# Turning normalised row tiles by transposing DMAs instead of array transposes and VectorE copies, with new planner tables

## The chip, the cores and the metric

The kernel runs on one core of one Trainium2 chip. Five engines work side by side, each through its own instructions in order: PE (TensorE, matmuls, with its weight loads shown as PEld), DVE (VectorE), ACT (ScalarE), POOL (GpSimd) and SP (SyncE, which here issues every DMA). The metric is the device time of one execution in microseconds, the median of several runs.

## The reference

Two layers of the same kind follow each other, with the same weights. Each adds softmax attention with 16 heads of width 28 to x, and then a feed-forward block with a squared relu; both read a layer norm of x without weights. x has 2048 rows of 448, the hidden width is 1792.

```python
x = x + _A_ref(_layernorm(x), A_wqkv, A_wo)
x = x + _B_ref(_layernorm(x), B_w1, B_b1, B_w2, B_b2)
x = x + _A_ref(_layernorm(x), A_wqkv, A_wo)
x = x + _B_ref(_layernorm(x), B_w1, B_b1, B_w2, B_b2)
# _A_ref: q, k, v = x @ wqkv; softmax(q @ k.T * 28**-0.5) @ v, per head; then @ wo
# _B_ref: relu(x @ w1 + b1)**2 @ w2 + b2
```

## The kernel before, in words

The 2048 rows are 16 row tiles of 128, mostly worked in blocks of two (256 rows). The attention is a long row of units: one unit is a score tile of 128 keys x r by 256 queries, 128x512 numbers in one PSUM bank, for one head. There are 2048 units in all. A score group (`s_stream`, matmuls at L1087) fills up to three banks of one of two PSUM buffers called sc, and one exp on ACT (`e_stream`, L1119) turns two or three banks of it into probabilities in `pts`. The matmuls at L1316 (`p_stream`) multiply them with V into oT.

Not all units go to ACT. Some are taken by DVE (`a_unit`, L1191: read the bank into v_w or K_sb), and the exponential is then worked out on POOL (L1216) and DVE (square at L1222, closing at L1255 in one instruction, or at L1243 after a further POOL instruction at L1231). I call this the side path. A unit of it takes 0.68 us of DVE for the first step alone, and the bank is not free for the next scores before that step is done.

Beside the units run the streams of the layers: for a finished block, the softmax's divisors go by small DMAs from SBUF (dn, L1420) to DRAM (scr, L1431) and back spread over rows (rec, L1439), the result is multiplied (L1444), projected and added to x (L1454), normalised, multiplied with w1 (relu L1512, square L1521) and w2, added, normalised again, and turned into the next layer's Q, K and V. All these matmuls but the transposes stand at L815 (`mm_tile`).

Each layer norm ends in the part that is changed. DVE writes the normalised row tile into one of four buffers xn (L779, two tiles make a pair, and two pairs take turns). PE transposes it, four 128x128 squares a tile, into a PSUM bank tp (L715), and DVE copies the bank into xnT (L727), where the features lie on the partitions and which is what L815 multiplies. xnT has three buffers; in the first layer's opening some blocks stand in K_sb of the other layer instead. PSUM is shared by two single banks (R_m), for which these transposes, the projections, the hidden layers and the oT sums stand in line. Where PE would have too little to do, `heat` (L1747) has it multiply ident with xn to no purpose.

The order on every engine is fixed when the program is built, by a planner (`Planner.run`): it keeps a clock for each engine, takes the operation that can start soonest, with priorities and with due times for scores and exps, and writes it into that engine's instructions. Tables of 128 numbers, one for each stretch of the run (OWN3, PACE, MIXT), decide how many units go to the side path, where in PSUM they lie, and which of the two closings they take. On the chip every engine then follows its own list, and a wait holds up all that stands behind it on that engine.

Of the kernel before, what the change touches and what calls it, by code (L numbers as in the profile page):

```python
# [14 lines left out]
P = 128  # L15
# [97 lines left out]
MIXT = (-9.0, 1.2, 1.2, -9.0, 1.2, 99.0, -9.0, 1.2, -9.0, 1.8, -9.0, -9.0, -9.0, 1.2, -9.0, 1.2, 1.8, -9.0, 1.8, 1.8, 1.2, 1.8, 1.8, -9.0, 1.2, 1.8, 1.2, -9.0, 1.2, -9.0, 1.2, 1.2, -9.0, -9.0, -9.0, 1.8, 1.8, -9.0, 1.8, -9.0, -9.0, -9.0, 1.2, 1.8, 1.2, 1.8, 1.8, -9.0, -9.0, 1.2, -9.0, 1.2, -9.0, 1.2, 1.2, -9.0, -9.0, -9.0, -9.0, -9.0, 1.2, 1.8, -9.0, -9.0, -9.0, 1.8, 1.2, 1.8, 1.2, -9.0, 1.2, 1.8, -9.0, 1.2, 1.2, 1.2, 1.2, 1.2, 1.8, -9.0, 99.0, 1.8, 99.0, 1.8, 99.0, 99.0, -9.0, 1.2, 1.2, 1.8, 1.8, 1.2, 1.2, 1.2, 1.8, 1.2, -9.0, 1.2, -9.0, -9.0, 1.8, 1.2, 1.2, 1.8, 1.8, 99.0, -9.0, 1.8, 99.0, -9.0, -9.0, -9.0, -9.0, 1.8, -9.0, 1.8, -9.0, 1.8, 1.8, 1.8, 1.2, -9.0, -9.0, 1.8, -9.0, -9.0, -9.0, -9.0)
# [20 lines left out]
EV = 2.9  # L134
# [244 lines left out]
def kernel(  # L379
# [12 lines left out]
    nc = tc.nc  # L392
    _, S, D = A_x.shape
# [27 lines left out]
    pl = Planner()  # L421
# [246 lines left out]
    def layernorm(t0, nt, deps_of, early=False, mv=None, place=None, x_in=None, parts=False):  # L668
# [34 lines left out]
        xnT = box["x"]  # L703
        ends = []
        todo = []

        def turn(p0, own, xs):
            box = {}

            def tr(e, xs=xs):  # L710
                tp = bank(t, "tp").bitcast(DT.bfloat16).rearrange("p (c q) -> p c q", c=NDC)
                box["t"] = tp
                for k, (xn, _) in enumerate(xs):
                    for dc in range(NDC):
                        nc.tensor.transpose(out=tp[:, dc, k * P:(k + 1) * P],  # L715
                                            in_=xn[:, dc * P:(dc + 1) * P], identity=ident[:, :])
            t = Op("PE", 0.07 * NDC * len(xs), tr, deps=[x[1] for x in xs],
                   acq=pools_now(early) if early else spare(1))
            yield t

            def ev(e, p0=p0, w=len(xs) * P):
                tp = box["t"]
                dst = xnT[:, :, p0 * P:p0 * P + w]
                if e == "ACT":
                    nc.scalar.copy(out=dst, in_=tp[:, :, 0:w])
                else:
                    return nc.vector.tensor_copy(out=dst, in_=tp[:, :, 0:w])  # L727
            o = Op("DVE", 0.15 + 0.265 * len(xs), ev, deps=[t], rel=t, sets=[("xT", t0 + p0)] if early else ())
            ends.append(o)
            pl.spawn(EV, iter([o, Op("DVE", 0.0, None, deps=[t], rel=own)]))  # L730

        if parts:
            own = Op("DVE", 0.0, None, acq=R_xn)
            yield own
            xn = xns[2 * (own.turn % 2)]
# [10 lines left out]
            for h, nm in enumerate(nms):  # L746
# [5 lines left out]
                t = Op("PE", 0.14, tr, deps=[nm], acq=spare(1) if h == 0 else None)  # L752
# [7 lines left out]
                o = Op("DVE", 0.28, ev, deps=[t], rel=box["o"])  # L760
# [5 lines left out]
        for p0 in range(0, nt, wide):  # L766
            js = range(p0, min(p0 + wide, nt))
            own = Op("DVE", 0.0, None, acq=R_xn)
            yield own
            xs = []  # L770
            for j in js:
                xn = xns[2 * (own.turn % 2) + j % 2]
# [16 lines left out]
            while todo:  # L789
                p0, own, xs = todo.pop(0)  # L790
# [158 lines left out]
    units = []  # L949
# [10 lines left out]
    at = [0]  # L960
# [60 lines left out]
    def s_stream():  # L1021
        while at[0] < len(units):
# [5 lines left out]
            def fn(e, gi=gi, us=us, js=js):  # L1028
# [174 lines left out]
    def a_rest(gi, c, box, unit):  # L1203
# [253 lines left out]
    def chain(l, qb):  # L1457
# [341 lines left out]
```

## Time and profile before

| | us |
|---|---|
| median of 3 runs | 809.45 (809.03 to 810.5) |
| span of the profiled execution | 808.2 |
| PE busy | 765.5 (95%) |
| DVE busy | 774.6 (96%) |
| ACT busy | 790.5 (98%) |
| POOL busy | 469.7 (58%) |

The profiled execution has a span of 808.2 us from its first instruction to its last; no time of its own beyond the span is given, and the runs are 0.8 to 2.3 us longer. In a row of the timeline the columns are start, duration, engine, line, operation and tiles; in brackets the engine's idle time before it and what ended that. In a group's row stand the count, the busy time and the mean duration of one in ns, and the idle time before. A row of waits has engine and line, the thing waited for, the total, the number of times and the longest, in us. A row of windows has, after the length, the busy time with the number of instructions for PE, PEld, DVE, ACT and POOL, then the clock, the DMA share and GB/s.

### The profile page before, as it was taken

What the parts mean: (1) busy time and instruction counts of PE and PEld (TensorE: products, weight loads), DVE (VectorE), ACT (ScalarE), POOL (GpSimd) and SP (SyncE); (2) the same over time, 40 slices, a digit from 0 to 9 for tenths busy, and PEclk for the clock granted to TensorE, in tenths of its full rate; (3) what the DMA queues carried; (4) which work ended last, traced back from release to release, by engine and by line L of the source; (5) the groups of instructions that cost most, each with busy time, mean ns of one, the idle gap of its engine ahead of it and who ended that gap; (6) DMA issues with size and microseconds to landing.
All of it is one profiled execution on the core that took longest, in us unless ns stands there. A gap on an engine that the chain in (4) does not pass through costs nothing.

```text
span 808.2 us, 27605 instructions
## 1 busy us (share of the span) xinstructions
PE 765.5 (95%) x11451; PEld 403.5 (50%) x11451; DVE 774.6 (96%) x1720; ACT 790.5 (98%) x683; POOL 469.7 (58%) x720
## 2 busy tenths in 40 slices
PE   8999989999999999999999999988999999998998
PEld 5555545454545545454445444444454544545655
DVE  7999999999999999999999999999999999999965
ACT  7999999999999999999999999999999999999994
POOL 3265666666576566665565676655566665666600
PEclk9999999999999999999999999999999999999999
DMA  9200010000000000000000000011100000000000
GB/s 254 78 2 2 17 29 16 15 17 17 6 11 16 16 15 16 5 13 15 2 2 3 2 2 2 15 32 30 33 10 21 22 28 27 15 15 16 21 15 13
DMA packets 32366, 17.94 MB, mean 22 GB/s; under 512 B 17833, under 2 KB 31787, under 8 KB 32240
## 3 DMA queue, kind: packets, MB, share of 16 engines
q1 hardware_dynamic: 32240, 16.18, 7.2%
q8 instruction: 89, 1.46, 0.7%
q14 instruction: 37, 0.30, 0.1%
HBM read 13.88 MB, written 2.07 MB: 20 GB/s over the span
## 4 chain that ended last, share of the span: by engine, by line
PE 36%; DVE 30%; ACT 22%; issue 9%; POOL 1%; DMA 1%; ACTq 0%; DVEq 0%; POOLq 0%
ACT pts L1119 22%; PE mt L815 16%; PE sc L1087 11%; DVE v_w L1191 6%; PE oT L1316 6%; DVE K_sb L1191 2%; DVE pts L1243 2%; DVE pts L1222 2%; DVE r L1512 2%; DVE V_sb L1243 2%; DVE st L657 2%; DVE V_sb L1222 2%; DVE x_sb L1454 1%; DMA dn<-oT_sb 1%; DVE Q_sb L834 1%
## 5 line engine op out<-in xcount | busy, mean ns | idle before, releaser
L1119 ACT ACTIVATE pts<-sc 128x1536 bf16<-128x1536 f32 (+1 forms) x668 | 780.4, 1336 | 2.9 <-PE sc L1087 2.0
L1087 PE MATMUL sc<-Q_sb,K_sb 32*128 32x256 bf16 (+1 forms) x4370 | 273.6, 265 | 27.6 <-ACT pts L1119 22.1
L1087 PEld LDWEIGHTS <-K_sb 32*128 32x128 bf16 x4478 | 104.6, 92 | 197.7 <-issue 137.6
L1231 POOL TENSOR_SCALAR v_w<-v_w 128x512 int16<-128x512 f32 x211 | 140.9, 668 | 67.2 <-DVE V_sb L1243 8.4
L1316 PE MATMUL oT<-pts,V_sb 128*32 128x256 bf16 (+1 forms) x3996 | 153.7, 268 | 0.8 <-ACT pts L1119 0.3
L1191 DVE TENSOR_SCALAR v_w<-sc 128x512 f32<-128x512 f32 x199 | 135.0, 680 | 2.7 <-PE sc L1087 2.0
L815 PE MATMUL mt<-xnT,w 128*128 128x256 bf16 (+1 forms) x888 | 116.6, 271 | 3.9 <-DVE x_sb L1454 0.8
L1216 POOL TENSOR_SCALAR pts<-v_w 128x512 bf16<-128x512 uint16 x113 | 78.5, 695 | 63.7 <-DVE v_w L1191 31.4
L1316 PEld LDWEIGHTS <-V_sb 128*32 128x32 bf16 x4352 | 90.6, 96 | 49.5 <-issue 38.5
L815 PEld LDWEIGHTS <-w 128*128 128x128 bf16 x896 | 76.5, 97 | 36.7 <-issue 28.0
L1216 POOL TENSOR_SCALAR V_sb<-v_w 128x512 bf16<-128x512 uint16 x94 | 66.9, 712 | 45.9 <-DVE v_w L1191 18.7
L1512 DVE TENSOR_SCALAR r<-mt 128x512 bf16<-128x512 f32 x108 | 73.3, 680 | 2.4 <-PE mt L815 1.8
L1231 POOL TENSOR_SCALAR K_sb<-K_sb 128x512 int16<-128x512 f32 x88 | 60.4, 687 | 25.4 <-DVE pts L1243 2.5
L815 PE MATMUL mt<-w,V_sb 128*128 128x448 bf16 (+2 forms) x288 | 68.9, 346 | 0.0
L1222 DVE TENSOR_TENSOR pts<-pts 128x512 bf16<-128x512 bf16 (+1 forms) x118 | 60.4, 512 | 0.1
L1191 DVE TENSOR_SCALAR K_sb<-sc 128x512 f32<-128x512 f32 x82 | 55.5, 680 | 0.7 <-PE sc L1087 0.4
L1222 DVE TENSOR_TENSOR V_sb<-V_sb 128x512 bf16<-128x512 bf16 (+1 forms) x103 | 52.3, 508 | 0.0
L1243 DVE TENSOR_TENSOR pts<-pts,v_w 128x512 int16<-128x512 bf16 (+1 forms) x95 | 43.6, 459 | 1.1 <-DVE pts L1222 0.5
L1216 POOL TENSOR_SCALAR pts<-K_sb 128x512 bf16<-128x512 uint16 x43 | 30.0, 697 | 23.2 <-DVE K_sb L1191 9.4
L1454 DVE TENSOR_TENSOR x_sb<-x_sb,mt 128x448 bf16<-128x448 bf16 x61 | 37.0, 608 | 2.7 <-PE mt L815 2.2
L657 DVE BATCH_NORM_STATS2 st<-x_sb 128x6 f32<-128x448 bf16 x63 | 38.5, 614 | 0.7 <-DMA x_sb<-in_A_x_dram 0.7
L815 PEld LDWEIGHTS <-V_sb 128*128 128x128 bf16 x302 | 24.5, 97 | 25.4 <-issue 12.1
(152 smaller groups left out, 923.8 us busy)
## 6 DMA issues: line engine op xcount, KB each, us to landing
rec<-scr SPq DMA_DIRECT2D x54, 128.0 KB
x_sb<-in_A_x_dram SPq DMA_DIRECT2D x8, 224.0 KB
out_dram<-x_sb SPq DMA_DIRECT2D x15, 112.0 KB
w<-in_B_w_dram SPq DMA_DIRECT2D x1, 1568.0 KB
w<-in_B_w_dram SPq DMA_DIRECT2D x1, 1344.0 KB
dn<-oT_sb SPq DMA_DIRECT2D x54, 4.0 KB
V_sb<-in_A_wqkv_dram SPq DMA_DIRECT2D x4, 168.0 KB
scr<-dn SPq DMA_DIRECT2D x27, 8.0 KB
```

Of the source, the lines that this page charges most:

```text
L657: return nc.vector.bn_stats(out=box["st"][:, :], in_=x_sb[:, t0 + j, :] if src is None else src())
L815: nc.tensor.matmul(box["t"][:, c0:c0 + n], lhsT=lhsT() if callable(lhsT) else lhsT, rhs=rhs, start=a, stop=b)
L1087: nc.tensor.matmul(dst[k][:, i * nt * P:(i + 1) * nt * P], lhsT=K_sb[l][rows, g, (kb + i) * P:(kb + i + 1) * P], rhs=Q_sb[rows, g, t0 * P: ...
L1119: t = nc.scalar.activation(out=pt[:, 0:n], in_=gbuf[gi]["sc"][:, 0:n], func=AF.Exp, scale=float(np.log(2.0)) * 2.0 ** -FRAC)
L1191: t = nc.vector.tensor_scalar(out=box["w"], in0=two(src), scalar1=EXP_SHIFT, scalar2=EXP_LOW, op0=ALU.add, op1=ALU.max)
L1216: return nc.gpsimd.tensor_scalar(out=two(pd), in0=low, scalar1=-EXP_MID * 65536, scalar2=EXP_BEND, op0=ALU.add, op1=ALU.mult)
L1222: return nc.vector.tensor_tensor(out=pd, in0=pd, in1=pd, op=ALU.mult)
L1231: return nc.gpsimd.tensor_scalar(out=two(box["t"]), in0=box["w"], scalar1=EXP_BITS, scalar2=1.0, op0=ALU.add, op1=ALU.mult)
L1243: return nc.vector.tensor_tensor(out=pd.bitcast(DT.int16), in0=pd, in1=t, op=ALU.add)
L1316: nc.tensor.matmul(box["t"][DHP * hh:DHP * hh + DHP, 0:n], lhsT=V_sb[l][:, kb + i, 4 * g + hh, :], rhs=p[:, c0:c0 + n], start=begin and kb ...
L1454: return nc.vector.tensor_tensor(out=x_sb[:, tb, lo:hi], in0=x_sb[:, tb, lo:hi], in1=t[:, 0:hi - lo], op=ALU.add)
L1512: return nc.vector.tensor_scalar(out=r[:, 0:w], in0=t[:, 0:w], scalar1=0.0, scalar2=None, op0=ALU.max)
```

## The change

A new stream `turned_by` issues, for a pair of tiles, two DMAs on SP that read xn and write the transposed tile straight into xnT (or K_sb). `turn` uses it wherever the block is neither one of the first three (`early`) nor the split last one (`parts`) and more than TSTOP = 40 units are left; otherwise PE and DVE turn the tile as before. The planner reckons 1.3 us for a tile on its DMA clock, and 0.5 us beside its usual 2.0 until the reader may start; the xn pair is free for the next normalisation when the DMAs are done. The three tables have new numbers all over.

```diff
-OWN3 = (0.0, 0.0, 0.0, 1.0, 0.0, 1.0, 0.0, 0.0, ...
+OWN3 = (0.0, 0.0, 0.0, 0.0, 1.0, 1.0, 0.0, 1.0, ...
-PACE = (0.6, 4.0, 2.6, 1.0, 3.4, 0.6, 2.2, 1.8, ...
+PACE = (3.0, 3.0, 3.0, 1.4, 4.0, 4.0, 2.2, 3.0, ...
-MIXT = (-9.0, 1.2, 1.2, -9.0, 1.2, 99.0, -9.0, ...
+MIXT = (1.2, 1.2, 1.8, 1.2, 1.2, 1.2, -9.0, ...
+TURN = 1.3
+TLAT = 0.5
+TSTOP = 40
...
+        def turned_by(p0, own, xs):
+
+            def by(e, p0=p0, xs=xs):
+                for k, (xn, _) in enumerate(xs):
+                    q = (p0 + k) * P
+                    t = nc.sync.dma_start(out=xnT[:, :, q:q + P], in_=xn[:, :], transpose=True)
+                return t
+            o = Op("DMA", TURN * len(xs), by, deps=[x[1] for x in xs], lat=TLAT)
+            ends.append(o)
+            yield o
+            yield Op("DVE", 0.0, None, deps=[o], rel=own)
+
         def turn(p0, own, xs):
+            if not early and not parts and len(units) - at[0] > TSTOP:
+                pl.spawn(EV, turned_by(p0, own, xs))
+                return
             box = {}
```

What the planner makes of it, in the program's order: 28 pairs (56 tiles) are turned by DMA, 2 pairs and 3 single tiles stay on the array. ACT has 285 exps of two banks and 384 of three (281 and 387 before), 1722 units for 1723; the side path has 326 units (325), of which 8 are closed at L1255 (24) and the others at L1243. PE has 95 filler matmuls for 71.

The first place is on DVE, late in the second layer. A pair of tiles is normalised, and before, the copy of the transposed tiles follows a few instructions later; K_sb, v_w, V_sb, pts and h are buffers of the side path, oT_sb the attention's sum.

```order
1513 L779 TENSOR_SCALAR xn_105<-x_sb,mv,rstd 128x448
1514 L1191 TENSOR_SCALAR K_sb_99<-sc 128x2x256
1515 L1343 COPY oT_sb<-oT 128x256
1516 L779 TENSOR_SCALAR xn_106<-x_sb,mv,rstd 128x448
1517 L1222 TENSOR_TENSOR V_sb_102<-V_sb_102 128x512
1518 L1454 TENSOR_TENSOR x_sb<-x_sb,mt 128x448
1519 L1243 TENSOR_TENSOR V_sb_102<-V_sb_102,v_w 128x512
1520 L727 COPY xnT<-tp 128x1024
```

In the changed kernel the same stretch (lines from L710 on stand 18 higher) reads:

```order
1483 L797 TENSOR_SCALAR xn_105<-x_sb,mv,rstd 128x448
1484 L1209 TENSOR_SCALAR K_sb_99<-sc 128x2x256
1485 L797 TENSOR_SCALAR xn_106<-x_sb,mv,rstd 128x448
1486 L1240 TENSOR_TENSOR V_sb_102<-V_sb_102 128x512
1487 L1261 TENSOR_TENSOR V_sb_102<-V_sb_102,v_w 128x512
1488 L1361 COPY oT_sb<-oT 128x256
1489 L1209 TENSOR_SCALAR K_sb_99<-sc 128x2x256
```

The copy is gone, DVE goes on with the side path, and the pair now reaches xnT through SP.

The second place is SP's list in the first layer. Before, it holds only the rounds of the divisors there: dn from the attention's sum, scr to DRAM, rec back.

```order
52 L1420 DMA dn<-oT_sb 128x1x8 x2
53 L1431 DMA scr_6795<-dn 128x2x8
54 L1439 DMA rec<-scr_6795 128x1x256 x2
55 L1420 DMA dn<-oT_sb 128x1x8 x2
56 L1431 DMA scr_7324<-dn 128x2x8
```

```order
82 L715 DMA_TRANSPOSE xnT<-xn_105 128x4x128
83 L715 DMA_TRANSPOSE xnT<-xn_106 128x4x128
84 L1438 DMA dn<-oT_sb 128x1x8 x2
85 L1449 DMA scr_7208<-dn 128x2x8
86 L715 DMA_TRANSPOSE xnT<-xn_107 128x4x128
87 L715 DMA_TRANSPOSE xnT<-xn_108 128x4x128
88 L1457 DMA rec<-scr_7208 128x1x256 x2
```

Transposes now stand between the rounds, and at five places, this one among them, inside a round.

How far the reader of xnT stands behind the normalisation can be counted in both orders. I count in exps: from the last exp that must be over before the pair's second tile is normalised and, after, its DMA may be issued (followed through all waits) to the last exp whose scores stand ahead of the first matmul that reads the pair, less one. I call this the lead. Before, at the first place above, the second tile's lead is 4. After, the 28 pairs have these leads:

| lead of the pair, in exps | 6 | 7 | 8 | 9 | 10 | 11 | 14 | 16 | 20 |
|---|---|---|---|---|---|---|---|---|---|
| pairs | 1 | 6 | 2 | 7 | 4 | 3 | 2 | 1 | 2 |

The pair of the first place is the one with lead 6.

More of the change, by code (lines that the diff above doesn't have):

```diff
@@ L98 @@
 V_PAST = 5
-OWN3 = (0.0, 0.0, 0.0, 1.0, 0.0, 1.0, 0.0, 0.0, 0.0, 0.0, 0.0, 1.0, 0.0, 1.0, 0.0, 0.0, 1.0, 0.0, 1.0, 0.0, 1.0, 1.0, 1.0, 1.0, 0.0, 1.0, 0.0, 1.0, 0.0, 1.0, 1.0, 0.0, 1.0, 1.0, 0.0, 0.0, 0.0, 0.0, 0.0, 1.0, 0.0, 0.0, 0.0, 1.0, 0.0, 1.0, 0.0, 1.0, 1.0, 0.0, 1.0, 0.0, 0.0, 0.0, 0.0, 0.0, 0.0, 0.0, 0.0, 0.0, 0.0, 0.0, 0.0, 1.0, 1.0, 1.0, 0.0, 1.0, 1.0, 0.0, 1.0, 0.0, 1.0, 0.0, 1.0, 0.0, 0.0, 0.0, 1.0, 0.0, 1.0, 1.0, 0.0, 0.0, 1.0, 0.0, 0.0, 1.0, 0.0, 0.0, 0.0, 0.0, 0.0, 0.0, 0.0, 0.0, 0.0, 1.0, 1.0, 0.0, 1.0, 0.0, 1.0, 0.0, 1.0, 0.0, 0.0, 1.0, 1.0, 1.0, 1.0, 0.0, 0.0, 0.0, 1.0, 0.0, 0.0, 1.0, 1.0, 1.0, 0.0, 0.0, 0.0, 0.0, 1.0, 1.0, 1.0, 1.0)
+OWN3 = (0.0, 0.0, 0.0, 0.0, 1.0, 1.0, 0.0, 1.0, 0.0, 0.0, 0.0, 0.0, 1.0, 0.0, 1.0, 1.0, 0.0, 0.0, 0.0, 0.0, 1.0, 1.0, 0.0, 1.0, 1.0, 1.0, 0.0, 0.0, 0.0, 0.0, 1.0, 0.0, 0.0, 1.0, 0.0, 1.0, 0.0, 0.0, 0.0, 0.0, 0.0, 1.0, 0.0, 1.0, 0.0, 0.0, 0.0, 1.0, 0.0, 1.0, 0.0, 1.0, 0.0, 0.0, 0.0, 0.0, 1.0, 1.0, 1.0, 1.0, 0.0, 0.0, 0.0, 0.0, 0.0, 0.0, 0.0, 1.0, 1.0, 1.0, 0.0, 1.0, 0.0, 1.0, 1.0, 0.0, 0.0, 0.0, 0.0, 0.0, 0.0, 0.0, 1.0, 0.0, 0.0, 1.0, 1.0, 0.0, 0.0, 0.0, 1.0, 0.0, 0.0, 1.0, 0.0, 1.0, 1.0, 0.0, 0.0, 0.0, 0.0, 0.0, 1.0, 0.0, 0.0, 0.0, 0.0, 0.0, 1.0, 1.0, 1.0, 1.0, 0.0, 0.0, 0.0, 0.0, 1.0, 1.0, 0.0, 0.0, 0.0, 0.0, 0.0, 0.0, 0.0, 0.0, 0.0, 0.0)
 FIRST = 50
@@ L113 @@
[L113 removed]
+PACE = (3.0, 3.0, 3.0, 1.4, 4.0, 4.0, 2.2, 3.0, 3.0, 3.0, 2.2, 3.4, 3.0, 2.2, 3.4, 1.4, 3.4, 3.0, 2.2, 3.0, 3.0, 2.2, 3.0, 1.4, 2.2, 3.0, 3.0, 3.0, 3.4, 1.4, 3.0, 3.0, 3.0, 3.0, 2.2, 4.0, 3.0, 3.4, 3.0, 4.0, 3.0, 3.0, 2.2, 4.0, 3.0, 3.0, 3.0, 3.0, 3.0, 2.2, 3.0, 4.0, 3.0, 3.0, 3.0, 4.0, 2.2, 2.2, 2.2, 3.0, 3.0, 1.4, 3.0, 3.0, 4.0, 2.2, 2.2, 3.0, 3.0, 3.0, 3.0, 1.4, 3.0, 3.0, 3.4, 3.4, 2.2, 4.0, 3.0, 3.0, 3.0, 3.0, 3.0, 3.0, 3.0, 3.4, 3.0, 4.0, 3.0, 2.2, 4.0, 3.0, 2.2, 4.0, 4.0, 3.0, 4.0, 2.2, 3.0, 3.0, 3.0, 3.0, 3.0, 2.2, 3.0, 3.0, 2.2, 3.0, 2.2, 3.0, 3.0, 2.2, 1.4, 3.0, 3.0, 2.2, 3.0, 3.0, 3.0, 3.0, 3.0, 3.0, 3.0, 3.0, 3.0, 3.0, 3.0, 3.0)
@@ new lines @@
+MIXT = (1.2, 1.2, 1.8, 1.2, 1.2, 1.2, -9.0, -9.0, 1.2, 1.2, -9.0, 1.2, 1.2, -9.0, 1.2, 1.8, -9.0, -9.0, -9.0, 1.2, 1.2, -9.0, 1.2, 1.2, 1.2, 1.2, 1.2, 1.2, 1.8, 1.2, 1.2, 1.2, -9.0, 1.8, 1.2, 1.8, 1.2, 1.2, 1.2, 1.2, 1.2, 1.2, 1.8, 1.2, 1.2, 1.8, 1.2, 1.2, 1.8, -9.0, -9.0, 1.2, 1.2, 1.2, 1.2, 1.2, 1.2, 1.8, 1.8, 1.2, 1.8, 1.2, 1.2, 1.2, 1.8, 1.2, 1.2, 1.2, -9.0, 1.2, 1.8, -9.0, 1.2, 1.2, 1.2, 1.2, 1.2, 1.2, 1.2, 1.2, 1.2, 1.2, 1.2, 1.8, 1.8, 1.2, -9.0, 1.2, 1.2, 1.2, 1.2, -9.0, 1.2, -9.0, 1.2, 1.8, 1.2, -9.0, 1.2, 1.2, 1.2, 1.2, -9.0, -9.0, -9.0, 1.2, 1.2, 1.2, 1.2, 1.2, 1.2, -9.0, 1.2, 1.2, 1.2, 1.8, 1.8, 1.2, 1.2, 1.2, 1.2, 1.2, 1.2, 1.2, 1.2, 1.2, 1.2, 1.2)
```

1 line of the change is left out of this document (removed).

## The prediction

> **What bounds the kernel now.** I read the page's busy line and chain first, then ACT's groups by form, the waits, three windows and a few stretches of the timeline.
>
> ```profile
> span 808.2 us, 27605 instructions
> PE 765.5 (95%) x11451; PEld 403.5 (50%) x11451; DVE 774.6 (96%) x1720; ACT 790.5 (98%) x683; POOL 469.7 (58%) x720
> ACT  7999999999999999999999999999999999999994
> ...
> PE 36%; DVE 30%; ACT 22%; issue 9%; POOL 1%; DMA 1%; ACTq 0%; DVEq 0%; POOLq 0%
> ```
>
> ACT is busy 98% of the span and only its first and last slices have room. The chain wanders over PE, DVE and ACT because the three hand each other small pieces; the engine that is never free is ACT. What ACT does:
>
> ```profile
> L1119 ACT ACTIVATE pts<-sc 128x1536 bf16<-128x1536 f32 x387 | 549.9, 1514 | 1.7 <-PE sc L1087 1.2 <-ACT pts L1119 0.2
> L1119 ACT ACTIVATE pts<-sc 128x1024 bf16<-128x1024 f32 x281 | 288.2, 1089 | 1.2 <-PE sc L1087 0.8 <-PE oT L1316 0.2
> L1119 ACT ACTIVATE pts<-sc 128x1536 bf16<-128x1536 f32 (+1 forms) x668 | 780.4, 1336 | 2.9 <-PE sc L1087 2.0 <-ACT pts L1119 0.2 <-PE oT L1316 0.2
> 11.66 5.48 ACT L1119 ACTIVATE pts<-sc 128x1536 bf16<-128x1536 f32 x4 [0.61 <-PE sc L1087]
> 783.46 10.89 ACT L1119 ACTIVATE pts<-sc 128x1536 bf16<-128x1536 f32 x8
> 787.45 6.90 ACT L1119 ACTIVATE pts<-sc 128x1536 bf16<-128x1536 f32 x5
> ```
>
> The reader is to see three things. The exponentials cover 780.4 us. They run from 11.66 to 787.45 + 6.90 = 794.35, which is 782.7 us, so 11.7 us of start and 13.9 us of end lie outside them. And an unhindered exp of three score tiles takes (787.45 - 783.46)/3 = 1.33 us; one of two tiles is 1514 - 1089 = 425 ns cheaper, 0.905 us. At that pace all of them would need 387 x 1.33 + 281 x 0.905 = 769.0 us. So 13.7 us is all that smoother feeding could ever give; the exponentials themselves are the floor.
>
> VectorE is the second engine:
>
> ```profile
> 100.00:200.00 100.00, 93.98 (x1387) 48.60 (x1387) 98.93 (x211) 99.80 (x86) 65.51 (x97) 1.00 0.07 19
> 300.00:400.00 100.00, 95.86 (x1367) 49.45 (x1366) 97.88 (x214) 99.88 (x87) 62.23 (x96) 1.00 0.04 10
> PEld L1087 <- DVE v_w L1191: 12.6, 38, 0.9
> PE sc L1087 <- ACT pts L1119: 22.1, 56, 0.9
> ```
>
> DVE is over 97% busy in the middle (the third pair of columns), and the loads for score matmuls wait for it to free a score bank (12.6 us behind the first step of the side path alone). PE waits for ACT 22.1/56 = 0.4 us at a time: that is the usual cover when PE is late.
>
> **The change, part by part.**
>
> *Array transposes and their copies.* 28 of the 30 pairs of row tiles lose eight transposes on PE and one copy on DVE.
>
> ```profile
> L727 DVE COPY xnT<-tp 128x1024 bf16<-128x1024 bf16 x26 | 17.6, 678 | 0.0
> 720.31 0.62 PE L715 MATMUL tp<-ident,xn 128*128 128x128 bf16 x8
> L1747 PE MATMUL mt<-xn,ident 128*128 128x448 bf16 x71 | 21.0, 356 | 1.0 <-DVE oT_sb L1345 0.4 <-DVE oT_sb L1343 0.3
> ```
>
> DVE: 28 x 0.678 = 19.0 us less. PE: 28 x 0.62 = 17.4 us less, but the program now holds 95 filler matmuls of L1747 for 71, at 21.0/71 = 0.30 us: 7.1 us back. Neither engine is the floor, so the direct worth is the idle time around these instructions:
>
> ```profile
> L715 PE MATMUL tp<-ident,xn x244: 216/219/230, 14.3 to 779.0; 128*128 128x128 bf16 x122
> ...
>   DVE r L1512: 0.9, 3
>   DVE xn L779: 0.8, 3
>   DVE v_w L1191: 0.4, 2
>   DVE x_sb L1454: 0.4, 1
>   DVE Q_sb L1521: 0.2, 1
> ```
>
> ```profile
>   PE mt L815: 1.0, 3
>   PEld L1087: 1.0, 3
> ```
>
> PE stood 2.7 us ahead of the transposes (the first list), and PE and its loads stood 2.0 us for the copy (the second list, who waited for L727). That is 4.7 us of PE idle. Between nothing reaching ACT and, at most, the 13.7 us above, I take half of the 4.7, since PE's own idle becomes ACT's only where no filled score bank is left: -2.4 us.
>
> *Tables.* Counted in the program's order, ACT gets 285 exps of two tiles and 384 of three instead of 281 and 387, so 1722 score tiles for 1723: 4 x 0.905 - 3 x 1.33 = -0.4 us on the floor. So almost nothing of DVE's freed time is spent on taking tiles off ACT. DVE closes a side-path tile with one scalar-tensor-tensor (L1255) 8 times instead of 24; the other way (L1243) is cheaper for it and costs POOL one instruction more. With one more tile (0.68 + 0.42 + 0.42) DVE ends at 774.6 - 19.0 - 16 x (0.682 - 0.415) + 1.5 = about 753 us. POOL has 18 more instructions of 0.67 us, 12.0 us, and is 58% busy: hidden.
>
> ```profile
> L1255 DVE SCALAR_TENSOR_TENSOR V_sb<-v_w,V_sb 128x512 int16<-128x512 f32 x9 | 6.1, 682 | 0.0
> L1243 DVE TENSOR_TENSOR V_sb<-V_sb,v_w 128x512 int16<-128x512 bf16 x69 | 28.7, 415 | 0.5
> L1231 POOL TENSOR_SCALAR v_w<-v_w 128x512 int16<-128x512 f32 x211 | 140.9, 668 | 67.2 <-DVE V_sb L1243 8.4 <-DVE pts L1243 7.4 <-DVE xn L779 5.0
> ```
>
> The 67.2 us of idle ahead of L1231 is that cover; without it, the 12.0 us would come back in part as waits of DVE.
>
> *The transposes on SP.* 56 new DMAs, two per pair, each turning one 128x512 tile (128 KB). The trace has no such DMA. The nearest rows:
>
> ```profile
> 93.16 1.16 SPq L1439 DMA_DIRECT2D rec<-scr  x2
> 94.37 1.18 SPq L1420 DMA_DIRECT2D dn<-oT_sb  x2
> 95.01 3.65 DMA dn<-oT_sb
> 98.69 0.25 DVE L1425 RECIPROCAL dn<-dn 128x16 f32<-128x16 f32 x1 [0.16 <-DMA dn<-oT_sb]
> 99.19 0.68 DVE L1444 TENSOR_TENSOR oTn<-oT_sb,rec 128x512 bf16<-128x512 f32 x1
> ```
>
> A small DMA from SBUF to SBUF, the second of a pair, takes 3.65 us from its issue until DVE may go on; two 128 KB ones (rec) were usable at 99.19 at the latest, 6.0 us after the first was issued. So a pair takes between 3.65 and 6.0 us from the second row tile's normalisation to both landings. I take 5.0: the bytes are those of rec, but its 6.0 is an upper limit in which the multiplication also waited its turn on DVE.
>
> How much is there? At one place of the kernel before:
>
> ```profile
> 719.48 0.46 DVE L779 TENSOR_SCALAR xn<-x_sb,mv,rstd 128x448 bf16<-128x448 bf16 x1
> 721.06 0.68 DVE L727 COPY xnT<-tp 128x1024 bf16<-128x1024 bf16 x1
> 721.79 1.03 PE L815 MATMUL mt<-xnT,w 128*128 128x256 bf16 x8 [0.15 <-DVE xnT L727]
> ```
>
> The second tile is normalised at 719.94 and the first reader starts at 721.79, 1.85 us later, with a lead of 4 exps in the order (the lead is explained with the change above). One more exp of lead is 780.4/668 = 1.17 us. So in the new order a lead of 6 gives 4.2 us, 7 gives 5.4, 8 gives 6.5, 9 gives 7.7, 10 gives 8.9, 11 gives 10.0. At 5.0 us only the pair with lead 6 is late, by 0.8, of which the 0.4 us cover takes half: +0.4 us. At 6.0 us it is 1.8 + 6 x 0.6 = 5.4 us less 7 x 0.4: +2.6 us. At 3.65 nothing.
>
> What is queued behind: SP runs in order, so dn, scr, rec and the stores stand behind transposes that wait for DVE's normalisation; at five places a pair stands inside a dn-scr-rec round (one is shown above). PE's matmuls on xnT wait for both DMAs, and all of PE's scores stand behind them. DVE's normalisation of the pair after next waits until xn is read; pairs lie some 10 exps or more apart for most of the run, so this costs nothing unless a pair takes over 10 us. The first DMA pairs stand between the weight loads on SP, with leads of 7 to 20, and w2 is read only by the first hidden layer: nothing.
>
> The Trainium skill is of two minds here. Its page "Advanced Engine Details and Errata", section X-Bar Transpose (TRN2), says transposing DMAs are as fast as plain ones; by that the rec rows hold and the sum stays. Its page "VectorE: DVE Perf Modes", section The three transpose paths, gives 1309 ns for a 128x128 through the DMA crossbar against 390 on TensorE; an estimate from it, eight squares in turn, is 10.5 us a pair, and the sum would be about 870 us. No run here shows either; it is the fourth rival.
>
> *Start and end.* Both keep the array: the first three blocks, and the last row tiles. The last exp has two tiles instead of three (in the 0.4 already). Nothing else.
>
> **The sum.** 809.45 - 0.4 - 2.4 + 0.4 = 807.0 us, from the median of the runs; the profiled span of 808.2 lies 1.25 below that median, and the same 1.25 is taken to lie around the new span of about 805.8.
>
> **The rivals.**
>
> 1. *The freed time isn't used.* The waits that go only move to the next late thing on PE. For it: ACT's whole idle before exps is 2.9 us. Against: DVE at 98% is what PE's loads wait for, and it falls by 20 us. Time: 809.45 - 0.4 + 0.4 = 809.4.
> 2. *Slower: the second transpose starts only when the first has landed.* The price is then 2 x 3.65 = 7.3 us a pair. Against: the two dn DMAs overlap (94.37 to 98.69 is 4.3 us for both). Late: lead 6 by 3.1, six pairs of lead 7 by 1.9, two of lead 8 by 0.8: 16.1 us, less 9 x 0.4: +12.5 us, 819.1 from 807.0 less its 0.4. It decides from about 5.8 us a pair upward, where lead 7 loses its cover; in between lie 810 to 819.
> 3. *SP's order.* At the five mixed rounds rec comes later by the pair's issue and its wait, some 2 us; DVE, which never waited for rec (no idle stands before L1444), then stands, and half reaches ACT: +5 us, 812.
> 4. *Squares in turn.* Each 128x512 tile is turned as four squares, one after another. At the shortest DMA trip of this trace, scr issued at 91.58 and rec let go at 93.16, 1.58 us, that is 12.6 us a pair: late at leads 6 to 11, 121 us less 23 x 0.4, about 919 us.
>
> ```profile
> 91.58 0.39 SPq L1431 DMA_DIRECT2D scr<-dn  x1
> ```
>
> **How the numbers follow.** Forecast 0.45, rival 1 0.15, rival 2 0.28, rival 3 0.07, rival 4 0.05. A measurement of this kernel tells 0.2%, 1.6 us, from no change. Faster: the forecast, 0.45. Same: rival 1, 0.15. Slower: rivals 2 to 4, 0.40. The forecast's own range is 803.5 (5.5 us of the 13.7 regained) to 809.2 (+2.6 instead of +0.4, and nothing more). The range to 818 takes in rival 3 and most of rival 2; beyond it stay rival 4 and the upper third of rival 2, below it some 0.03.
>
> **What would show it.** L727's group shrinks to about 5 copies and DVE to about 753 us; ACT's exps stay near 780 us; SP shows 56 transposes at L715. If the forecast is right, PE's waits for a DMA transpose (PE or PEld at the first-layer and QKV matmuls) total under 1 us, and a pair lands within 5.4 us. Rival 2 shows as PE waiting for transposes by 1 to 3 us at some nine places and ACT idle behind PE; rival 3 as DVE idle before the multiplication with rec. The prediction fails if a pair takes over 6 us, or if the new order has a wait of its own elsewhere, which the order alone does not tell.

## The result and the profile after

The changed kernel takes 819.4 us (median) against 809.3 us for the kernel before on the same chip: a ratio of 1.0121, with a 95% interval from 1.0104 to 1.0137. It is slower, by 10 us; 807.0 had been forecast.

The page of the changed kernel (busy times, clock by slices, chain) begins:

```profile
span 816.2 us, 27439 instructions
...
PE 761.3 (93%) x11305; PEld 391.7 (48%) x11305; DVE 767.1 (94%) x1691; ACT 792.3 (97%) x685; POOL 476.2 (58%) x738
...
PEclk9899999999999999999999999999999999999999
...
PE 33%; DVE 29%; ACT 23%; issue 9%; DMA 3%; POOL 2%; SPq 0%; DVEq 0%; ACTq 0%; POOLq 0%
```

Its exps, by form, and in the second fence the first and the last stretch of them in the timeline (lines from L723 on of the new kernel stand 18 higher, so L1119 is now L1137):

```profile
L1137 ACT ACTIVATE pts<-sc 128x1536 bf16<-128x1536 f32 x384 | 549.8, 1507 | 8.8 <-PE sc L1105 5.4 <-PE oT L1334 2.4 <-ACT pts L1137 0.5
L1137 ACT ACTIVATE pts<-sc 128x1024 bf16<-128x1024 f32 x285 | 293.7, 1080 | 1.4 <-PE sc L1105 0.8
```

```profile
10.56 6.82 ACT L1137 ACTIVATE pts<-sc 128x1536 bf16<-128x1536 f32 x5 [0.61 <-PE sc L1105]
...
788.55 13.19 ACT L1137 ACTIVATE pts<-sc 128x1536 bf16<-128x1536 f32 x10
```

The exps run from 10.56 to 801.74 us, 791.2 us against 782.7 before. At the prediction's pace they would need 384 x 1.33 + 285 x 0.905 = 768.6 us, so the floor has stayed (769.0 before) and the time that ACT loses beside it has grown from 13.7 to 22.6 us. PE and DVE did become less busy, by 4.2 and 7.5 us, and that bought nothing. Two signs are new: a slice with a lower clock at the start (the second is at 0.8, where all stood at 0.9 or more before), and DMA with 3% of the chain for 1%.

The clock leads to one place, where one piece of the chain's DMA time lies too. (The chain's other DMA pieces are two rounds of scr and rec, and one pair of transposes that comes back below.) The timeline of the changed kernel at 28 to 44 us, on four engines:

```profile
27.96 5.24 SPq L715 DMA_TRANSPOSE K_sb<-xn  x4
...
34.41 0.42 DVE L1363 TENSOR_TENSOR K_sb<-oT,K_sb 128x256 f32<-128x256 f32 x1 [2.77 <-DMA K_sb<-xn]
34.89 0.40 PE L1334 MATMUL oT<-pts,V_sb 128*32 128x256 bf16 x8 [2.18 <-DVE K_sb L1363]
35.36 1.45 ACT L1137 ACTIVATE pts<-sc 128x1536 bf16<-128x1536 f32 x1 [2.14 <-PE oT L1334]
...
39.70 1.45 ACT L1137 ACTIVATE pts<-sc 128x1536 bf16<-128x1536 f32 x1 [0.91 <-PE sc L1105]
...
42.31 2.79 ACT L1137 ACTIVATE pts<-sc 128x1536 bf16<-128x1536 f32 x2 [1.16 <-PE sc L1105]
```

In the opening, partial sums of the attention are kept in the other layer's K_sb: DVE copies one in at L1361 and adds the next at L1363. The turned tiles of blocks 3 to 5 go to the same buffer, into other columns (by the code, 0 to 1023 for the tiles and 1024 to 2047 for the sums). Before, DVE wrote both, in its own order. Now SP's DMAs write the tiles, and the addition on DVE waits until four of them have landed. PE waits for the addition, which frees its bank, and ACT for PE. What follows is in the windows of the changed kernel (after the length, busy us and counts of PE, PEld, DVE, ACT and POOL, then the clock, the DMA share and GB/s), in the first fence; the second has two windows of the kernel before:

```profile
28.00:32.00 4.00, 3.84 (x48) 1.77 (x41) 3.63 (x8) 4.00 (x5) 1.56 (x3) 1.00 0.31 71
32.00:36.00 4.00, 1.11 (x18) 0.51 (x16) 1.59 (x5) 1.86 (x2) 1.22 (x3) 0.90 0.54 127
36.00:40.00 4.00, 3.92 (x36) 1.57 (x35) 2.82 (x9) 2.56 (x3) 0.62 (x1) 0.50 0.99 296
40.00:44.00 4.00, 4.00 (x55) 1.61 (x52) 3.20 (x9) 2.84 (x3) 0.00 (x0) 0.75 0.30 101
```

```profile
32.00:36.00 4.00, 3.73 (x61) 2.10 (x63) 4.00 (x12) 4.00 (x5) 2.44 (x5) 1.00 0.00 0
36.00:40.00 4.00, 3.79 (x62) 2.03 (x57) 4.00 (x11) 4.00 (x4) 0.00 (x0) 1.00 0.01 4
```

PE was busy for 1.11 us of the second window. In finer windows its clock falls to 0.50 at about 35.2 us and is back at 1.00 at 42.0, so the 0.75 of the last row is two us of each. In these 6.8 us PE was busy for 6.0, but at half speed. ACT lost 2.14 us to the wait and then, with the clock at half, 1.44 and 1.16 us more: of 12 us it worked 1.86 + 2.56 + 2.84 = 7.26, where it worked all the time before. The Trainium skill's page "TensorE: Matmul & The Clock Gate", section Part 1: The HAM clock gate (the "warmup" mystery), has the clock fall to half after an idle window of about 3.4 us. The trace agrees in part only: PE had stood for 2.18 us at a stretch, with 1.11 us of work in the 4, so no whole window of 3.4 us was idle.

The transposes themselves are hardly waited for (the waits that end with a DMA into xnT, K_sb or rec: total, times, longest):

```profile
DVE K_sb L1363 <- DMA K_sb<-xn: 2.8, 1, 2.8
DVE oTn L1462 <- DMA rec<-scr: 1.6, 2, 1.3
PE mt L833 <- DMA xnT<-xn: 1.3, 1, 1.3
```

### The profile page after: what moved, and what is told of

Read it like the earlier page. It is cut to its first block, busy times and chain, and to the rows that moved or that the text cites. A ratio compares the mean times of both kernels' runs of the same rounds, so it can differ in the third digit from the quotient of the medians.

```text
span 816.2 us, 27439 instructions
## 1 busy us (share of the span) xinstructions
PE 761.3 (93%) x11305; PEld 391.7 (48%) x11305; DVE 767.1 (94%) x1691; ACT 792.3 (97%) x685; POOL 476.2 (58%) x738
## 3 DMA queue, kind: packets, MB, share of 16 engines
q8 instruction: 88, 1.44, 0.8%
## 4 chain that ended last, share of the span: by engine, by line
PE 33%; DVE 29%; ACT 23%; issue 9%; DMA 3%; POOL 2%; SPq 0%; DVEq 0%; ACTq 0%; POOLq 0%
ACT pts L1137 23%; PE mt L833 15%; PE sc L1105 10%; PE oT L1334 5%; DVE v_w L1209 5%; DVE r L1530 3%; DVE pts L1240 2%; DVE V_sb L1240 2%; DVE pts L1261 2%; DVE K_sb L1209 2%; DVE st L660 2%; DVE V_sb L1261 2%; DVE x_sb L1472 1%; DMA rec<-scr 1%; DVE oTn L1462 1%
## 5 line engine op out<-in xcount | busy, mean ns | idle before, releaser
L1137 ACT ACTIVATE pts<-sc 128x1024 bf16<-128x1024 f32 (+1 forms) x669 | 781.6, 1325 | 10.2 <-PE sc L1105 6.2
L1105 PE MATMUL sc<-Q_sb,K_sb 32*128 32x256 bf16 (+1 forms) x4442 | 276.8, 266 | 32.7 <-ACT pts L1137 27.8
L1249 POOL TENSOR_SCALAR v_w<-v_w 128x512 int16<-128x512 f32 x225 | 149.0, 662 | 72.5 <-DVE pts L1261 16.9
L833 PE MATMUL mt<-xnT,w 128*128 128x256 bf16 (+1 forms) x888 | 118.9, 271 | 6.2 <-DVE r L1530 2.0
L833 PE MATMUL mt<-w,V_sb 128*128 128x448 bf16 x274 | 68.6, 355 | 0.0
L1240 DVE TENSOR_TENSOR pts<-pts 128x512 bf16<-128x512 bf16 (+1 forms) x120 | 63.5, 530 | 0.0
L1209 DVE TENSOR_SCALAR K_sb<-sc 128x512 f32<-128x512 f32 x85 | 57.7, 679 | 1.5 <-PE sc L1105 1.2
L1240 DVE TENSOR_TENSOR V_sb<-V_sb 128x512 bf16<-128x512 bf16 (+1 forms) x108 | 55.2, 511 | 0.4 <-POOL V_sb L1234 0.4
L1261 DVE TENSOR_TENSOR V_sb<-V_sb,v_w 128x512 int16<-128x512 bf16 (+1 forms) x82 | 37.0, 453 | 0.8
```

The lines of the kernel that those rows point to most:

```text
L833: nc.tensor.matmul(box["t"][:, c0:c0 + n], lhsT=lhsT() if callable(lhsT) else lhsT, rhs=rhs, start=a, stop=b)
L1105: nc.tensor.matmul(dst[k][:, i * nt * P:(i + 1) * nt * P], lhsT=K_sb[l][rows, g, (kb + i) * P:(kb + i + 1) * P], rhs=Q_sb[rows, g, t0 * P: ...
L1137: t = nc.scalar.activation(out=pt[:, 0:n], in_=gbuf[gi]["sc"][:, 0:n], func=AF.Exp, scale=float(np.log(2.0)) * 2.0 ** -FRAC)
L1209: t = nc.vector.tensor_scalar(out=box["w"], in0=two(src), scalar1=EXP_SHIFT, scalar2=EXP_LOW, op0=ALU.add, op1=ALU.max)
L1240: return nc.vector.tensor_tensor(out=pd, in0=pd, in1=pd, op=ALU.mult)
L1249: return nc.gpsimd.tensor_scalar(out=two(box["t"]), in0=box["w"], scalar1=EXP_BITS, scalar2=1.0, op0=ALU.add, op1=ALU.mult)
```

## The experiments

### Where the turned tiles of the opening lie

```diff
+    def place_of_block(blk):
+        if blk == 2:
+            return K_sb[1][:, :, 0:QR]
+        if 3 <= blk <= 5:
+            r = {3: 8, 4: 10, 5: 6}[blk]
+            return V_sb[1][:, r:r + 2, :, :].rearrange("p t h r -> p (t h r)").rearrange("p (c q) -> p c q", c=NDC)
...
-                                            place=K_sb[1][:, :, (blk - 2) * QR:(blk - 1) * QR] if 2 <= blk <= 5 else None)
+                                            place=place_of_block(blk))
```

> The changed kernel with one edit: the turned tiles of blocks 3, 4 and 5 land in unused rows of the second layer's V_sb instead of K_sb, so that the opening's partial sums, which lie in K_sb too, and the transposing DMAs no longer wait for each other; the order on every engine stays. Theory A (the mutual wait in K_sb and the clock that falls behind it cost most of the 10 us): DVE's wait of 2.8 us for a transpose is gone, the granted clock is 1.00 between 32 and 44 us, ACT's exps lose 5 us less, and the time is 811 to 813. Theory B (the new order, that is the tables, costs it): the wait goes, the time stays at 816 or more. Theory C (transposing DMAs are late everywhere): 816 or more, with PE waiting for transposes at many places.

It took 814.4 us, a ratio of 1.0054 (1.0039 to 1.0069), between the theories. So the wait in K_sb, with the half clock behind it, cost 5.0 us, half of the loss, and another half is left. The idle time of ACT in the stall, 2.14 + 1.44 + 1.16 = 4.74 us, is nearly all of it; how much of it the clock alone made, no run separates. The windows of this kernel show the stall gone, with a full clock:

```profile
32.00:36.00 4.00, 3.82 (x60) 2.16 (x58) 4.00 (x12) 4.00 (x4) 2.12 (x4) 1.00 0.94 279
36.00:40.00 4.00, 3.87 (x63) 1.72 (x66) 4.00 (x11) 4.00 (x4) 0.00 (x0) 1.00 0.73 180
```

In its timeline one pair is late, at 303 us (the same pair as in the changed kernel):

```profile
295.23 1.12 SPq L1465 DMA_DIRECT2D rec<-scr  x2
...
296.47 2.53 SPq L715 DMA_TRANSPOSE xnT<-xn  x2
...
303.43 0.60 PE L833 MATMUL mt<-xnT,w 128*128 128x256 bf16 x4 [1.81 <-DMA xnT<-xn]
...
304.46 1.45 ACT L1145 ACTIVATE pts<-sc 128x1536 bf16<-128x1536 f32 x1 [1.10 <-PE sc L1113]
```

This pair, issued 1.2 us behind two rec DMAs, took 303.43 - 296.47 = 7.0 us. That rec made it so is not shown: in the same run a pair issued at 149.63, as close behind its rec DMAs, was read at 155.40 without a wait, within 5.8 us. Nor did the clock fall here: PE stood 1.81 us, and the windows from 300 to 306 us have it at 1.00.

### One part of the change alone

Three kernels undo a part each and let the planner make its order anew. The first keeps the new tables and turns the opening's pairs on the array:

```diff
+        mv_given = mv is not None
...
-            if not early and not parts and len(units) - at[0] > TSTOP:
+            if mv_given and not parts and len(units) - at[0] > TSTOP:
```

> The changed kernel with the five first-layer opening pairs (blocks 3 to 7) turned on the array again, planned anew with the new tables; 23 pairs still go by DMA. Theory A: 811 to 813, clock 1.00 throughout. Theory B: 816 or more. Theory C: 816 to 819, since 23 of 28 pairs remain.

The second is the kernel before with the new OWN3, PACE and MIXT:

```diff
-OWN3 = (0.0, 0.0, 0.0, 1.0, 0.0, 1.0, ...
+OWN3 = (0.0, 0.0, 0.0, 0.0, 1.0, 1.0, ...
```

> The kernel before with the three new tables alone and no transposing DMA. Theory A: within 3 us of the kernel before, 808 to 812. Theory B: 816 or more. Theory C: 808 to 812.

The third is the changed kernel with the old tables:

```diff
-OWN3 = (0.0, 0.0, 0.0, 0.0, 1.0, 1.0, ...
+OWN3 = (0.0, 0.0, 0.0, 1.0, 0.0, 1.0, ...
```

> The changed kernel with the three old tables: all transposing DMAs, among them the three pairs in K_sb, planned with the old numbers. Theory A: slower than before by 5 to 12 us, 814 to 821, with DVE's wait for a transpose into K_sb and a dip of the clock before 50 us. Theory B: 809 to 812. Theory C: 816 to 821 with PE waiting for transposes at many places.

They took 862.2 us (1.0642, from 1.0605 to 1.0679), 838.7 (1.0359, from 1.0342 to 1.0375) and 855.1 (1.0560, from 1.0534 to 1.0585). No theory had foreseen this size; where one said 816 or more, the number lies 22 to 46 us above that. The exps' groups of the three, in this order:

```profile
L1138 ACT ACTIVATE pts<-sc 128x1536 bf16<-128x1536 f32 (+1 forms) x668 | 784.8, 1324 | 49.8 <-PE sc L1106 26.9
```

```profile
L1119 ACT ACTIVATE pts<-sc 128x1536 bf16<-128x1536 f32 (+1 forms) x671 | 785.9, 1327 | 24.6 <-PE oT L1316 15.3
```

```profile
L1137 ACT ACTIVATE pts<-sc 128x1536 bf16<-128x1536 f32 (+1 forms) x669 | 785.4, 1326 | 41.4 <-PE oT L1334 17.5
```

The number of exps and their busy time are nearly those of before (668 and 780.4); ACT's idle time is not, 25 to 50 us for 2.9. The likely reason is that the tables' numbers belong to one order each: an operation of another length moves everything behind it in the plan, and the numbers then meet other units. So these three say nothing on what the DMAs or the tables are worth, and from here on I kept an order and changed only what the instructions in it do. One of them still shows a price. The first kernel's longest stall, on three engines:

```profile
530.43 0.70 DVE L798 TENSOR_SCALAR xn<-x_sb,mv,rstd 128x448 bf16<-128x448 bf16 x2 [1.08 <-POOL rstd L689]
530.90 2.50 SPq L716 DMA_TRANSPOSE xnT<-xn  x2
534.67 1.87 PE L834 MATMUL mt<-xnT,wk 128*128 128x256 bf16 x8 [9.05 <-DMA xnT<-xn]
```

With nothing ahead of it in the queue, a pair takes 534.67 - 530.90 = 3.8 us; the rest of PE's 9.05 us is that the normalisation came late.

### The new order, with plain DMAs

```diff
                 for k, (xn, _) in enumerate(xs):
                     q = (p0 + k) * P
-                    t = nc.sync.dma_start(out=xnT[:, :, q:q + P], in_=xn[:, :], transpose=True)
+                    if place is None:
+                        t = nc.sync.dma_start(out=xnT[:, :, q:q + P], in_=xn[:, :].rearrange("p (c q) -> p c q", c=NDC))
+                    else:
+                        t = nc.sync.dma_start(out=xnT[:, :, q:q + P], in_=xn[:, :], transpose=True)
```

> The order of e1_own_place, kept, with the 50 transposing DMAs of the later pairs replaced by plain DMAs of the same 128x512 tile between the same buffers and with the same waits. The turning is left out, so the matmuls read unturned rows. A, the transposes cost what the one late pair at 303 us costs (ScalarE stood 1.1 us there) and are hidden elsewhere: 814.4 becomes 812.5 to 814.5. C, the transposing DMA's own length (1.22 us of SP for one, 3.6 to 7 us for a pair) is what is left of the loss: 811 or less.

It took 813.1 us, 1.0041 (1.0029 to 1.0053): 1.3 us less than with the turning, where A had put it, though the two intervals overlap. SP needs half as long for a DMA. The issues of the pairs, in ns (least, median, most), in the changed kernel and in this one:

```profile
L715 SPq DMA_TRANSPOSE xnT<-xn x50: 1188/1220/2102, 48.4 to 763.3; - x50
```

```profile
L716 SPq DMA_DIRECT2D xnT<-xn x50: 593/637/1247, 39.9 to 756.3; - x50
```

And the pair that was late, in the timeline, is not waited for as a DMA any more:

```profile
295.56 1.38 SPq L716 DMA_DIRECT2D xnT<-xn  x2
...
301.11 0.60 PE L836 MATMUL mt<-xnT,w 128*128 128x256 bf16 x4 [0.39 <-DVE x_sb L1483]
```

Its only wait for a DMA behind the opening is for rec, in the list of waits:

```profile
DVE oTn L1473 <- DMA rec<-scr: 1.0, 1, 1.0
```

So turning costs SP twice the time of a plain copy of the same tile, and the kernel about 1 us, if that. Some 3 to 4 us of loss against before are in the new order and the plain DMAs together. One part of it can be seen, and no DMA of a row tile lies near it: two rounds of the divisors now follow each other directly, and the second scr, issued at 94.00 us right behind the first round's two rec DMAs (from 92.69), needs 3.54 us to land, where the first round's, at 90.80, needed 1.88; before, the rounds at this place were 7 us apart. DVE's wait of 1.0 us for rec stands behind it, and then ACT (the first row is from the chain, issue and time to landing, the second from the timeline):

```profile
94.00 3.54 DMA scr<-dn
105.67 1.45 ACT L1148 ACTIVATE pts<-sc 128x1536 bf16<-128x1536 f32 x1 [0.86 <-PE sc L1116]
```

The same 0.86 us stands in the changed kernel at 110.68 and in the one with the tiles in their own place at 106.27. ACT's idle time ahead of all exps is 2.9 us before, 4.6 here, 5.9 with the turning and 10.2 with the tiles in K_sb.

### The order before, without the freed work

```diff
-            box["x"] = xtp.tile([P, NDC, QR], DT.bfloat16, name="xnT") if place is None else place
+            if place is not None:
+                box["x"] = place
+            elif early or parts or len(units) - at[0] <= 60 or len(olds) < 3:
+                box["x"] = xtp.tile([P, NDC, QR], DT.bfloat16, name="xnT")
+                olds.append(box["x"])
+            else:
+                box["x"] = olds[own_xt.turn % 3]
+                box["kept"] = True
...
-                for k, (xn, _) in enumerate(xs):
-                    for dc in range(NDC):
+                for k, (xn, _) in enumerate(xs[:1] if kept else xs):
+                    for dc in range(1 if kept else NDC):
                         nc.tensor.transpose(out=tp[:, dc, k * P:(k + 1) * P],
...
+                if kept:
+                    return nc.vector.tensor_copy(out=xnT[:, 0, p0 * P:p0 * P + 8], in_=tp[:, 0, 0:8])
```

> The kernel before with its own tables and its own order, kept; of the later pairs' eight array transposes one stays, and the copy shrinks from 128x1024 to 128x8, so that most of the 28 x 0.68 us of VectorE and 28 x 0.62 us of TensorE go while nothing comes in their place (the rest of those row tiles keeps the data of an earlier pair). A, the prediction's step: taking this work away is worth some 2.4 us, 807. B, by the slope of e5_copy_back (9.6 us for 17.1 us of VectorE, 0.56 us for one): 25 x 0.58 x 0.56 = 8 us, 801 or less. With B the loss of the change lies in the order that its tables make; with A the freed work was never worth much.

It took 809.1 us, 0.9997 (0.9988 to 1.0006). Neither A's 2.4 us nor B's 8: in the old order, the work that this run leaves out (24 of the 28 copies, and seven of eight transposes each) was worth nothing that can be measured. Its busy times, then the groups of the copies and of one closing of the side path, then the last exps in the timeline:

```profile
PE 757.3 (94%) x11283; PEld 395.3 (49%) x11283; DVE 769.8 (95%) x1720; ACT 790.8 (98%) x683; POOL 471.1 (58%) x720
```

```profile
L732 DVE COPY xnT<-tp 128x8 bf16<-128x8 bf16 x24 | 3.6, 151 | 0.0
...
L1253 DVE TENSOR_TENSOR V_sb<-V_sb,v_w 128x512 int16<-128x512 bf16 x69 | 29.4, 426 | 0.5
```

```profile
784.75 9.56 ACT L1129 ACTIVATE pts<-sc 128x1536 bf16<-128x1536 f32 x7
```

The last exp ends at 784.75 + 9.56 = 794.31 us; before, at 794.35. 24 copies lost 24 x (0.678 - 0.151) = 12.6 us, yet DVE's busy time fell by only 4.8: other instructions of DVE became longer, the closings of the side path (before at L1243, 415 ns in the prediction's row) among them, by 11 ns here.

### The other way: work added

The new order, with the turned tiles in their own place, and a statistic on DVE for each pair:

```diff
                     t = nc.sync.dma_start(out=xnT[:, :, q:q + P], in_=xn[:, :], transpose=True)
+                st = sp.tile([P, 6], DT.float32, name="st")
+                nc.vector.bn_stats(out=st[:, :], in_=x_sb[:, t0, :])
                 return t
```

> The order of e1_own_place, kept, with 28 statistics of 0.61 us (BATCH_NORM_STATS2 of a 448-wide row, 0.61 us in the trace) put back on VectorE, one at each place where a pair is handed to the DMA queue: 28 x 0.61 = 17.1 us, about the 19.0 us that the copies took. Their results are read by nobody. A, VectorE's freed time is hardly used, since the exponentials are the floor and the order doesn't take tiles off ScalarE: e1's 814.4 us rises by 0 to 3, to 814 to 818. B, the new order lives on the freed time (it is cut as tight as the order before was): a rise of over 8 us, 822 or more.

The order before, with the same statistics behind the array transposes:

```diff
                         nc.tensor.transpose(out=tp[:, dc, k * P:(k + 1) * P],
                                             in_=xn[:, dc * P:(dc + 1) * P], identity=ident[:, :])
+                if not early:
+                    st = sp.tile([P, 6], DT.float32, name="st")
+                    nc.vector.bn_stats(out=st[:, :], in_=x_sb[:, t0, :])
```

> The kernel before with its own order, kept, and 28 statistics of 0.616 us more on VectorE, one behind each pair's transposes: 17.2 us of VectorE, as many as e5_copy_back added to the new order. A, an order made to fit is one-sided: taking work out of it gave nothing (e8_no_copy: 0.9997), but adding work costs as much as in the new order, some 0.56 us for one, so 809.4 becomes 817 to 821. B, the order before has room of some 13 us on both sides, as its unmoved time without the copies could also mean: 812 or less. With B the new order is the tighter of the two and has spent the freed time; with A the two are cut alike.

824.0 us (1.0196, from 1.0166 to 1.0226; its six runs lie between 821.6 and 830.3) and 822.2 us (1.0158, from 1.0141 to 1.0175). For the first that is B's 822 or more; the second lies 1.2 us above A's range, and far from B's. The added groups of the two, each with its exps:

```profile
L717 DVE BATCH_NORM_STATS2 st<-x_sb 128x6 f32<-128x448 bf16 x28 | 17.2, 616 | 0.0
...
L1147 ACT ACTIVATE pts<-sc 128x1024 bf16<-128x1024 f32 (+1 forms) x669 | 784.7, 1313 | 12.6 <-PE sc L1115 9.8
```

```profile
L719 DVE BATCH_NORM_STATS2 st<-x_sb 128x6 f32<-128x448 bf16 x29 | 17.8, 614 | 0.0
...
L1122 ACT ACTIVATE pts<-sc 128x1536 bf16<-128x1536 f32 (+1 forms) x668 | 784.1, 1309 | 10.9 <-PE sc L1090 7.9
```

A microsecond more on DVE costs 9.6/17.2 = 0.56 us in the new order and 12.8/17.8 = 0.72 us in the old one. So A of the second expectation holds in its direction, with a steeper price than its 0.56: the old order, the only one tried both ways, is one-sided. DVE's busy time fell by only 4.8 us there when work was left out; at 0.56 to 0.72 us for one that would still have been some 3 us, and 0.2 was measured. A reading that fits, but that no run isolates: work that is added delays what stands behind it, and work that is taken out only lets engines wait earlier for the same exps. The surest use of the freed 19 us would be to take score tiles off ACT, and the new order takes one of 1723.

### Every transpose twice

```diff
+                    nc.sync.dma_start(out=xnT[:, :, q:q + P], in_=xn[:, :], transpose=True)
                     t = nc.sync.dma_start(out=xnT[:, :, q:q + P], in_=xn[:, :], transpose=True)
```

> The order of e1_own_place, kept, with every transposing DMA issued twice, so that a quiet pair takes 3.6 + 2 x 1.22 = 6.0 us and one behind a pair of rec DMAs some 9 us. A, the leads of 7 to 20 exps cover most of it: by the prediction's leads 2.6 us at 6.0 us a pair and some 3 us more for the pairs behind rec, 814.4 becomes 817 to 823. C, transposes are on the path nearly everywhere: 28 x 1.2 us or more, 848 or over would be all of it, and 830 or more half of it.

It took 899.8 us, 1.1110 (1.1087 to 1.1134). The timeline shows first that the price was not the one I had meant:

```profile
176.51 1.19 SPq L715 DMA_TRANSPOSE xnT<-xn  x1
...
179.19 1.19 SPq L716 DMA_TRANSPOSE xnT<-xn  x1
...
180.48 1.22 SPq L715 DMA_TRANSPOSE xnT<-xn  x1
...
182.81 1.19 SPq L716 DMA_TRANSPOSE xnT<-xn  x1
...
185.28 1.87 PE L834 MATMUL mt<-xnT,wk 128*128 128x256 bf16 x8 [3.13 <-DMA xnT<-xn]
```

The second DMA to the same place is held until the first has landed, 2.3 to 2.7 us after its issue, so a pair takes 185.28 - 176.51 = 8.8 us instead of 6.0, with waits much like those that the prediction's second rival meant. The waits:

```profile
PE mt L834 <- DMA xnT<-xn: 52.9, 16, 5.8
PEld L834 <- DMA xnT<-xn: 18.2, 6, 5.0
DVE oTn L1471 <- DMA rec<-scr: 8.4, 4, 2.6
DVE dn L1452 <- DMA dn<-oT_sb: 4.4, 2, 3.1
```

22 times PE or its loads stood for a transpose, 71 us in all, and the time rose by 899.8 - 814.4 = 85 us. By the prediction's leads, 8.8 us a pair would be late by 4.6 once, by 3.4 six times, by 2.3 twice and by 1.1 seven times, 37 us together, less half a cover each. The real stalls are twice that. SP then runs late with dn and rec too, as the last two rows show. And the clock falls again: its mean over this run is 0.951, against 0.999 with each transpose issued once, so part of the 85 us is PE at half speed behind its waits, and no run says how much. A's range is far off; the time passes C's 848, but at a dearer pair than C reckoned with. What holds is that this order covers its pairs but one as they are, and does not cover pairs of 9 us.

## Why the prediction was wrong, point by point

- **The floor.** The exps stayed the floor: their busy time is within 1% of 780.4 us in every run, whatever else was done (784 to 786 in the groups shown). That "13.7 us is all that smoother feeding could ever give" was true as a limit and misleading as a prospect: without the freed work, ACT lost as much beside its exps as before.
- **Array transposes and their copies, -2.4 us.** Mis-sized: 0, between -1.0 and +0.5 us by the interval of the run that leaves the work out in the old order. The 4.7 us of idle time around these instructions was PE's and no loss of ACT, whose whole idle time before its exps was 2.9 us by the prediction's own row; taking half of it was a guess. Rival 1's mechanism, that the freed time isn't used, was the right one for this part; its 809.4 failed on the parts below.
- **Tables, -0.4 us, DVE at about 753 us.** The count of units was right, and it should have been read as a warning: the new order spends the freed time on nothing that the floor feels. DVE came to 767.1 us for the 753 forecast: other instructions of it became longer (the squares from pts, L1240, 453 ns for 427 before). With plain DMAs, the new order stands at 1.0041 where the old one without the freed work stands at 0.9997: the term that I set at -0.4 is some 4 us (813.1 less 809.1) with the plain DMAs' waits in it. One place of it is in the traces, the two rounds of divisors in a row, with DVE's wait of 1.0 us for rec and ACT's of 0.86; what the rest of this step consists of stays open.
- **"The first DMA pairs ... : nothing."** This is the step that failed worst. It looked at what SP has queued there, and at the readers of the tiles, but not at who else uses the buffer that the tiles land in. Before, one engine wrote both things in K_sb, and no wait could be seen; with two engines there is one, and 2.77 us of it cost 5.0 us, with the clock at half behind it. The prediction had named the case in general ("a wait of its own elsewhere") and given it no price.
- **The price of a pair, 5.0 us.** Between the two pairs that were waited for, and by luck: 3.8 us in a quiet queue and 7.0 behind two rec DMAs, or 3.5 and 6.6 counted as in the prediction, from the end of the second normalisation. The second is over the 6 us at which the prediction said that it fails. PE waited once, 1.3 us (1.8 with the tiles in their own place), against the forecast of under 1 us in all, and at 303 us, not at the pair with lead 6 (issued at 725 us), which alone had been forecast late. The turning costs 1.3 us of time (814.4 to 813.1), within the intervals, against the +0.4 forecast.
- **"Of which the 0.4 us cover takes half."** With every transpose held up, a late microsecond cost 85/71 = 1.2 us, not less than one, with the fallen clock in it. The 0.4 us of cover was read from the short waits of the trace before, and these are longer.
- **Rival 2, 819.1 us**, came within 0.3 us of the time by another way. The second transpose of a pair doesn't wait for the first to land (4 are issued in 5.24 us at 27.96, and one needs 2.3 us to land). With a wait of that kind forced twice on each pair, the kernel took 899.8 us.
- **Rival 3, SP's order,** happened at the size of one place or two: DVE waited 1.6 us in all for rec. At the one that can be followed, rec came late behind another round's DMAs and not behind transposes.
- **Rival 4, squares in turn,** is out: a pair of 128x512 tiles takes 3.8 us, where eight squares at the 1309 ns of the Trainium skill's page "VectorE: DVE Perf Modes", section The three transpose paths, would take 10.5 by an estimate. The Trainium skill's other page, "Advanced Engine Details and Errata", section X-Bar Transpose (TRN2), has a transposing DMA as fast as a plain one; that holds within 1.3 us for this kernel's time but not for SP, which was held 1.22 us for 0.64.

The ladder of medians, which the runs support, is: 809.3 before; 809.1 in the old order without the freed work; 813.1 in the new order with plain DMAs; 814.4 with transposing ones; 819.4 with the turned tiles in K_sb. The step from 813.1 to 814.4 is within the intervals. No run was faster than the kernel before by more than its interval.

## What to carry to other kernels

When work moves from one engine to another, look first at every other user of the buffers that it writes: what one engine's own order kept apart needs a wait as soon as there are two engines, and here a wait of 2.8 us in front of PE cost 5.0. Relieving an engine that isn't the floor was worth nothing in the kept order tried here, and to cost such an edit, ask which instruction of the bounding engine disappears. Where an order was fitted by tables, no part of a change can be judged by planning anew with tables of another plan; keep the order and change what its instructions do.

## What the runs showed of the hardware

- PE's clock fell to 0.50 at 35.2 us, just after PE had stood for 2.18 us, stayed there for 6.8 us with PE busy for 6.0 of them, and was at 1.00 again from 42.0 us on (0.90, 0.50 and 0.75 in the three windows of 4 us). After a gap of 1.81 us that ends at 303 us, in the kernel with the tiles in their own place, it stayed at 1.00.
- A transposing DMA of a 128x512 tile holds SP for 1.22 us, a plain one of the same bytes for 0.64 us. In a quiet queue the transposing one lands 2.3 us after its issue (the last fence, from the chain of the run with every transpose twice: start of the issue, time to landing). Behind two rec DMAs issued 1.2 us earlier one pair needed 7.0 us instead of 3.8, and another no more than 5.8; what made the difference was not tested.
- DVE's busy time isn't a sum that work can simply be taken from: 12.6 us of copies left and 4.8 us of busy time went, since others grew, the group shown by 11 ns each. Why they did was not tested.

```profile
182.81 2.34 DMA xnT<-xn
```
